# Fetching the next query tile back one step later, in a kernel whose SyncE queue carries copies and transposes alike

## The chip, the cores and the metric

The kernel runs on one core of one Trainium2 chip. The metric is the device time of one execution in microseconds (us). Times of a kernel are medians of several runs; profiles are single executions, and their span is about 2 us shorter than the device time of the same run.

The engines: PE is TensorE's matmul, PEld its weight loads, DVE is VectorE, ACT is ScalarE, POOL is GpSimd, SP or SPq is SyncE, which here issues almost every DMA from one queue.

## The reference, cut to what matters

One transformer block with linear attention, over 2048 tokens of width 576, 32 heads of 18:

```python
h = layernorm(x) * (1 + ca) + sa
q, k, v = heads(h @ wqkv)
phi_q = concat(softmax(q @ w_phi), softmax(-(q @ w_phi)))     # 36 features per head
phi_k = ...                                                   # the same of k
num = phi_q @ (phi_k^T v);  den = phi_q @ sum(phi_k)
x = x + ga * ((num / den) @ wo)
h = layernorm(x) * (1 + cb) + sb
x = x + gb * (relu(h @ w1) @ w2)                              # width 4608
```

The tokens are cut into 16 tiles of 128. The MLP at the end works on two tiles at a time: 8 blocks.

## The kernel before

First comes a phase that builds phi_k^T v and the query features of all tiles (up to some 91 us). Features of tiles 4 to 15 are not kept in SBUF until they are wanted: they are written to DRAM (`eqd`) and fetched back into a ring `EL` of NL = 3 buffers. Then the 8 MLP blocks run, each a first linear layer (`l1`, lines L673 and L680) and a second (`l2`, L735). The attention of tiles t+2 and t+3 is laced into the first layer of the block of tiles t and t+1.

What the change touches:

```python
NEQ, NE, NV, NL = 6, 5, 4, 3     # NL: buffers of the ring EL

def eq(u):                       # tiles 0..3 stay in SBUF, later ones live in the ring
    return EQ[:, SLOT[u], :] if u < QF else EL[:, u % NL, :]

def q_in(u):                     # L337: fetch of 288 KB, overwrites the buffer of tile u - 3
    sp.dma_start(EL[:, u % NL, :], eqd[:, u, :])

def q_turn(u):                   # L348: reads the buffer of tile u
    sp.dma_start_transpose(ET[:, u % NET], eq(u).rearrange("p (c f) -> p c f", f=P))

def q_fin(u):
    q_sm(u)                      # DVE: sums of the exponentials, reciprocal
    q_pool(u)                    # POOL: normalises in place
    q_turn(u)

def q_next(q):
    if q < NT:
        q_fin(q)
        if q + NL < NT:
            q_in(q + NL)         # waits, in the SyncE queue, for q_turn(q) just above

def attend(t):
    num_mm(t, pr)                # L389: matmuls on ET of tile t
    num_o(t, pr)                 # DVE: division, into o_sb
    if t > 1:
        act.activation(out=o_sb[:, t % 2, D:640], in_=o_sb[:, t % 2, 512:D], func=ACT.Copy)   # L795
    turn_dma(oT[:, t % 2], o_sb[:, t % 2, :])        # L401: transpose of the attention output
# wo_rest (L802) and wo_full (L808): matmuls on oT, by @ wo
```

Where the calls stand, block b with t0 = 2b + 2:

```python
# in l1 of block b
if (g, u) in (((0, 0), (1, "first")) if b == 1 else ((0, 0), (0, 2))):
    attend(t0 + int(u in (2, "first")))
if b == 0 and (g, u) == (1, "first"):
    q_next(t0 + 2)
if g and u == "rest":
    wo_rest(t0 + g - 1, pair(3))
# ... wo_full, residual, statistics, norm2 (a transpose of xn) ...
# in l2 of block b
if pos in ((4, 10) if b else (12,)):
    q_next(t0 + 2 + int(pos > 4))
# the output stores: L765 of tile t+1 ahead of pos 12, L769 of tile t behind it
```

So `q_next` is called for tile 4 in the first layer of block 0, for tile 5 at the end of block 0, for tiles 6 and 7 in the second layer of block 1, and so on, in pairs.

The softmax here doesn't subtract the row's maximum and nothing guards it: scores larger than these inputs give would overflow.

Of the kernel before, what the change touches and what calls it, by code (L numbers as in the profile page):

```python
# [17 lines left out]
NT = S // P  # L18
# [43 lines left out]
def tile_block(ctx, tc, a, out):  # L62
# [22 lines left out]
    NEQ, NE, NV, NL = 6, 5, 4, 3  # L85
# [250 lines left out]
    def q_in(u):  # L336
        sp.dma_start(EL[:, u % NL, :], eqd[:, u, :])  # L337
# [12 lines left out]
    def q_fin(u):  # L350
        q_sm(u)
        q_pool(u)
        q_turn(u)
# [427 lines left out]

    NB = NT // 2

    def q_next(q):
        if q < NT:
            q_fin(q)
            if q + NL < NT:
                q_in(q + NL)

    def attend(t):  # L790
        pr = pair(3)
# [25 lines left out]
    for b in range(NB):  # L817
# [3 lines left out]
        def in_l1(g, u):  # L821
            if not more:
                return
# [6 lines that stand above are left out]
            if g and u == 0:  # L830
                t = t0 + g - 1
                wo_full(t, pair(3))
                add_res(t, pair(3))
                bn(1, t)
            if (g, u) == (1, 2):
                norm2(b, t0)

        def in_l2(pos):
            if not more:
                return  # L840
            if pos == 1:
                norm2(b, t0 + 1)
            if pos == (8 if b else 12):
                hb = h2[:, (b + 1) % 2]
                for ci in range(NC):
                    dve.tensor_scalar(out=hb[:, ci, :], in0=hb[:, ci, :], scalar1=mod2[:, 1, ci:ci + 1],
                                      scalar2=mod2[:, 0, ci:ci + 1], op0=ALU.mult, op1=ALU.add)
            if pos in ((4, 10) if b else (12,)):
                q_next(t0 + 2 + int(pos > 4))
# [107 lines left out]
```

## Time and profile before

| | before |
|---|---|
| three runs, us | 389.54, 389.95, 391.97 (median 389.95) |
| span of the profiled run, us | 387.8 |
| TensorE busy, us | 380.5 (98%) |
| first layer of block 1, start to end, us | 23.33 |
| the same of blocks 2 to 5, us | 21.28 each |

The page and the views are read as follows. A line of the list of waits names the engine and line that waited, what ended the wait, then the total in us, the number of waits and the longest. A line of the timeline has the start, the length, the engine, the line of the kernel and what it writes from what. The length of an entry of SPq is the time in which SyncE issues the DMA; the data lands later (the fetch at 135.94 is issued in 0.33 us and lands 3.2 us after issue). The chain of waits goes back from the last instruction to what released each step. The granted clock is the share of TensorE's full clock that the trace records, as a mean over a window or a whole run: 1.00 is full speed, 0.50 is half.

The wait as TensorE has it, in its timeline:

```profile
137.88 0.83 PE L680 MATMUL PS<-h,R 64*128 64x256 bf16 x12
140.58 0.30 PE L802 MATMUL PS<-wo_sb,oT 64*128 64x288 bf16 x2 [1.87 <-DMA oT<-o_sb]
```

The twelve matmuls of L680 start at 137.88. What comes next in program order, L802, starts 2.70 us after that; the 1.87 us in brackets is idle time that ended when the DMA of oT landed.

### The profile page before, as it was taken

The page shows a single profiled execution, that of the slowest core. Times are in us where ns is not written, and L with a number is a line of the kernel's source. Part 1 is how long each engine was busy: PE and PEld are TensorE (multiplying, and loading weights), DVE is VectorE, ACT ScalarE, POOL GpSimd, SP SyncE. Part 2 cuts the span into 40 slices and gives each one's busy share as a digit, 9 for nine tenths or more (in the row PEclk, how much of TensorE's full clock was granted, in tenths as well). Part 3 has the DMA queues.
Part 4 walks back from the last instruction along what each step waited for, and adds up shares of the span by engine and source line. Part 5 has one row for each costly group of instructions (what it writes and reads, how often), then busy time and mean ns, then how long its engine had stood idle before and what let it go on. Part 6 is the DMA issues. An engine that isn't in the chain of part 4 may idle for free.

```text
span 387.8 us, 8927 instructions
## 1 busy us (share of the span) xinstructions
PE 380.5 (98%) x3705; PEld 310.3 (80%) x3705; DVE 242.7 (63%) x470; ACT 156.8 (40%) x380; POOL 125.3 (32%) x195
## 2 busy tenths in 40 slices
PE   8999999999999989999999999999999999999996
PEld 4887778888887868788888888887888788878885
DVE  2898998784897646735664485468365735552243
ACT  2689997687530233023302430341144114302510
POOL 2188889820107300530061026004500440042023
PEclk9999999999999999999999999999999999999999
DMA  7995799798520334151125104510530221200001
GB/s 296 421 417 207 275 379 362 134 260 290 67 63 19 47 79 35 33 137 28 29 63 108 36 19 91 96 19 19 123 36 19 45 64 36 35 0 33 3 0 33
DMA packets 48940, 43.18 MB, mean 111 GB/s; under 512 B 39297, under 2 KB 41986, under 8 KB 48130
## 3 DMA queue, kind: packets, MB, share of 16 engines
q1 hardware_dynamic: 48610, 42.41, 40.2%
q8 instruction: 29, 0.48, 0.5%
q10 hardware_dynamic: 288, 0.19, 0.2%
q14 instruction: 13, 0.11, 0.1%
HBM read 27.38 MB, written 5.90 MB: 86 GB/s over the span
## 4 chain that ended last, share of the span: by engine, by line
PE 90%; ACT 5%; DVE 2%; DMA 1%; issue 1%; POOL 1%; POOLq 0%; DVEq 0%; ACTq 0%
PE PS L673 32%; PE PS L735 31%; PE PS L272 11%; PE PS L680 5%; PE PS L808 4%; ACT RT L277 3%; PE PS L233 2%; PE PS L389 2%; PE PS L322 1%; DMA oT<-o_sb 1%; PE PS L249 1%; PE PS L406 1%; PE PS L802 0%; PE PS L257 0%; ACT RT L511 0%
## 5 line engine op out<-in xcount | busy, mean ns | idle before, releaser
L673 PE MATMUL PS<-h,R 128*128 128x256 bf16 x1152 | 132.1, 273 | 0.0
L673 PEld LDWEIGHTS <-R 128*128 128x128 bf16 x1152 | 111.6, 98 | 13.9 <-issue 0.6
L735 PEld LDWEIGHTS <-RH 128*128 128x128 f16 x846 | 82.8, 98 | 20.6
L721 POOL TENSOR_TENSOR yt<-yt,gb_row 128x288 f32<-128x288 f32 x23 | 28.0, 1219 | 204.7 <-DVE yt L720 204.7
L687 ACT ACTIVATE RH<-PS 128x256 f16<-128x256 f32 x72 | 27.5, 382 | 112.6 <-PE PS L680 92.3
L735 PE MATMUL PS<-R,RH 128*128 128x288 bf16 (+1 forms) x558 | 72.1, 286 | 0.0
L689 DVE SCALAR_TENSOR_TENSOR RH<-PS,RH 128x256 f16<-128x256 f32 x72 | 28.6, 412 | 61.0 <-ACT RH L687 61.0
L688 ACT ACTIVATE RH<-PS 128x512 f16<-128x512 f32 x72 | 42.9, 596 | 5.5 <-PE PS L673 4.6
L277 ACT ACTIVATE RT<-PS,rs 128x576 bf16<-128x576 f32 x64 | 42.8, 741 | 2.4 <-PE PS L272 1.8
L735 PE MATMUL PS<-RT,RH 128*128 128x288 f16 x288 | 37.9, 286 | 0.0
L739 ACT ACTIVATE RS<-PS 128x288 f32<-128x288 f32 x24 | 9.8, 410 | 65.2 <-PE PS L735 65.2
L272 PE MATMUL PS<-RH,R 116*128 116x288 bf16 x240 | 32.4, 286 | 0.0
L272 PE MATMUL PS<-RH,RT 116*128 116x288 bf16 x240 | 31.9, 286 | 0.3
L720 DVE TENSOR_TENSOR yt<-PS,RS 128x288 f32<-128x288 f32 x23 | 10.5, 455 | 31.0 <-PE PS L735 21.9
L238 DVE BATCH_NORM_STATS2 st<-x_sb 128x6 f32<-128x288 bf16 x64 | 25.9, 447 | 3.7 <-DMA x_sb<-in_xk_dram 3.1
L272 PEld LDWEIGHTS <-RT 116*128 116x128 bf16 x240 | 22.9, 98 | 6.0 <-issue 0.5
L272 PEld LDWEIGHTS <-R 116*128 116x128 bf16 x240 | 22.7, 98 | 5.9 <-issue 0.2
L722 POOL TENSOR_TENSOR x_sb<-yt,x_sb 128x288 bf16<-128x288 f32 x31 | 22.6, 731 | 2.9 <-DVE yt L718 1.1
L282 DVE TENSOR_REDUCE Rk<-RT 128x64 f32<-128x1152 bf16 x16 | 21.3, 1337 | 0.9 <-ACT RT L277 0.7
L282 DVE TENSOR_REDUCE Rq<-RT 128x64 f32<-128x1152 bf16 x16 | 21.5, 1344 | 0.0
L411 DVE TENSOR_TENSOR x_sb<-x_sb,PS 128x576 bf16<-128x576 bf16 x16 | 12.1, 753 | 13.4 <-PE PS L808 12.3
L680 PE MATMUL PS<-h,R 64*128 64x256 bf16 x288 | 19.9, 271 | 0.0
(119 smaller groups left out, 420.4 us busy)
## 6 DMA issues: line engine op xcount, KB each, us to landing
R<-in_w1a_dram SPq DMA_DIRECT2D x4, 1152.0 KB, 8.2
eqd<-RT SPq DMA_DIRECT2D x12, 288.0 KB, 2.1
RT<-eqd SPq DMA_DIRECT2D x12, 288.0 KB, 3.2
R<-in_w2b_dram SPq DMA_DIRECT2D x2, 1296.0 KB, 8.5
R<-in_w2a_dram SPq DMA_DIRECT2D x3, 864.0 KB
out_dram<-x_sb SPq DMA_DIRECT2D x15, 144.0 KB, 1.7
RT<-in_xT_dram SPq DMA_DIRECT2D x2, 640.0 KB, 13.9
x_sb<-in_xk_dram SPq DMA_DIRECT2D x3, 288.0 KB
```

The lines of the kernel that those rows point to most:

```text
L238: dve.bn_stats(out=s[:, hf, :], in_=x_sb[:, t, hf * HD:(hf + 1) * HD])
L272: pe.matmul(pr[:, k, 0:HD], lhsT=xt(t, ck), rhs=w[0:R, ck, k * HD:(k + 1) * HD], start=(ck == 0), stop=(ck == NC - 1))
L277: act.activation(out=E.rearrange("p (b h s e) -> p b h s e", b=2, s=2, e=DH)[:, :, :, s, :], in_=pr[:, :, 0:HD].rearrange("p b (h e) -> p ...
L282: dve.tensor_reduce(out=Rr, in_=E.rearrange("p (c e) -> p c e", e=DH), axis=AXX, op=ALU.add)
L673: pe.matmul(PS[:, 2 * u + hf, n * 256:n * 256 + 256], lhsT=w1a[:, ci, jj * P:(jj + 1) * P], rhs=hb[:, ci, :], start=(n == 0 and ci == 0), ...
L680: pe.matmul(PS[:, 2 * u + hf, n * 256:n * 256 + 256], lhsT=w1b[b0:b0 + 64, j * P:(j + 1) * P], rhs=hb[b0:b0 + 64, 4, :], start=False, stop ...
L687: act.activation(out=A11[:, j, :], in_=lo[:, :, 0, :], func=ACT.Relu)
L688: act.activation(out=A2[:, j, :, :], in_=PS[:, 2 * u + 1, :].rearrange("p (n s f) -> p n s f", n=2, s=2), func=ACT.Relu)
L689: dve.scalar_tensor_tensor(out=U3[:, j, :], in0=lo[:, :, 1, :], scalar=0.0, in1=A11[:, j, :], op0=ALU.max, op1=ALU.subtract)
L721: pool.tensor_tensor(out=y, in0=y, in1=gb_row[:, c], op=ALU.mult)
L722: pool.tensor_tensor(out=x_sb[:, t, c], in0=y, in1=x_sb[:, t, c], op=ALU.add)
L735: pe.matmul(PS[:, bank, 0:HD], lhsT=am[:, j, :], rhs=bm[:, j, :], start=first and j == 0, stop=(j % 9 == 8), skip_group_check=True)
```

## The change

The intent: the fetch of the next tile waits for the transpose of the present one, and the stores and transposes behind it in the SyncE queue wait with it. Fetched one call later, it finds its buffer free.

```diff
     NB = NT // 2
 
+    held = []
+
     def q_next(q):
+
+        if held and held[0] < NT:
+            q_in(held[0])
+        del held[:]
         if q < NT:
             q_fin(q)
-            if q + NL < NT:
-                q_in(q + NL)
+            held.append(q + NL)
```

## The prediction

> **What bounds the kernel now.** I read the page first, for which engine sets the end.
>
> ```profile
> span 387.8 us, 8927 instructions
> ...
> PE 380.5 (98%) x3705; PEld 310.3 (80%) x3705; DVE 242.7 (63%) x470; ACT 156.8 (40%) x380; POOL 125.3 (32%) x195
> ...
> PE 90%; ACT 5%; DVE 2%; DMA 1%; issue 1%; POOL 1%; POOLq 0%; DVEq 0%; ACTq 0%
> ```
>
> The reader is to see that TensorE is busy for 380.5 of 387.8 us. All that is not TensorE work is some 7.3 us, start-up and the last eviction and store included. A change that only moves DMA issues can win no more than what of those 7.3 us is a wait for a DMA. Which that is, the list of TensorE's waits over the whole run tells.
>
> ```profile
> PE PS L802 <- DMA oT<-o_sb: 1.9, 1, 1.9
> PE PS L233 <- POOL eps_t L225: 1.3, 1, 1.3
> PE PS L257 <- ACT RT L277: 0.2, 1, 0.2
> ```
>
> One wait in the MLP phase, 1.9 us, once: the first matmul of the output projection (L802) waits for the transposed attention output oT. Everything else there runs back to back. The same shows from another side when the first half of each MLP block (the first linear layer with the attention of two later tiles laced in) is put beside its like, with the busy times of the engines in windows cut at the block edges that the chain of waits gives:
>
> ```profile
> 91.25:112.60 21.35, 21.35 (x223) 17.91 (x222) 15.41 (x30) 11.11 (x25) 1.42 (x2) 1.00 0.59 142
> 128.03:151.36 23.33, 21.46 (x223) 17.85 (x221) 12.47 (x29) 8.35 (x21) 2.84 (x4) 1.00 0.46 60
> 166.79:188.07 21.28, 21.28 (x222) 17.87 (x221) 10.77 (x26) 8.36 (x21) 1.55 (x3) 1.00 0.35 80
> 203.50:224.78 21.28, 21.28 (x223) 17.86 (x221) 10.76 (x26) 8.36 (x21) 1.56 (x3) 1.00 0.34 66
> ```
>
> (The columns: window, its length, then busy time and count of PE, PEld, DVE, ACT and POOL, the granted clock, the DMA share, GB/s.) Block 1 takes 23.33 us, its like 21.28: 2.05 us more, at the same clock of 1.00. Blocks 2 to 5 are already equal to their TensorE work, to the hundredth. Last, the SyncE queue and its waits around that gap:
>
> ```profile
> 127.25 0.34 SPq L765 DMA_DIRECT2D out_dram<-x_sb  x1
> 131.32 1.29 SPq L348 DMA_TRANSPOSE RE<-RT  x1
> 135.94 0.33 SPq L337 DMA_DIRECT2D RT<-eqd  x1
> 136.36 0.39 SPq L769 DMA_DIRECT2D out_dram<-x_sb  x1
> 136.84 2.63 SPq L401 DMA_TRANSPOSE oT<-o_sb  x2
> ```
>
> ```profile
> SPq L337 <- DMA RE<-RT: 3.3, 1, 3.3
> ```
>
> This is the mechanism that the change is aimed at. At 131.32 SyncE issues the transpose of query tile 5 (L348). The next entry, the fetch of tile 8 (L337), overwrites the buffer that this transpose reads, so it waits 3.3 us for it. Behind it stand the output store L769 and the transpose of oT. The timeline shows the data of that oT ready much earlier: the last writer of o_sb (ACT, L795) runs from 133.55 for 0.26, to 133.81, and the store's data (POOL, L722) is there at 132.06 + 0.73 = 132.79. So oT was issued 136.84 - 133.81 = 3.0 us after its data, and TensorE, done with L680 soon after 138, had to wait until 140.58.
>
> [...] the 3.3 us stand in the SyncE queue and nothing behind is issued meanwhile. [...] the 0.33 us of L337 or 1.2 us of L401 aren't the transfer; for that I use the page's times from issue to landing (oT 2.6 median, 2.6 to 3.9; the query transpose 3.2 to 12.8, median 3.8; the fetch 2.7 to 3.6). [...] the granted clock is 1.00 in that window, so there is no second gain from a warmer clock.
>
> **The change part by part.** It removes nothing: the same twelve fetches of 288 KB, the same transposes, no instruction of a compute engine. It moves nine fetches (tiles 7 to 15) one call of q_next later, and puts them ahead of that call's own sums and transpose instead of behind them. The guard keeps fetches past tile 15 out.
>
> Call of tile 4 (block 0, SyncE at 103 us): its fetch, issued at 107.76, goes. Behind it stands a transpose of xn, issued at 109.14 and bound by its own data (xn is written from 108.48 for 0.64). No TensorE wait hangs on it: worth 0.
>
> Call of tile 5 (the end of block 0): now the fetch of tile 7 comes first. It waits for the transpose of tile 4, done since before 107.76, so it goes out right after the store at 127.25, at about 127.7, and by its landing time of 3.2 lands at about 131, before tile 5's transpose is issued. That transpose is bound by POOL (L289, 130.13 + 1.17 = 131.30) and stays at 131.32. Then no fetch. The store L769 goes at about 132.8, and oT at 133.83 instead of 136.84. With the landing of 2.6 to 3.9 it is there between 136.4 and 137.7. TensorE wants it at: L680 starts at 137.88, and in block 2 L802 starts 177.31 - 176.64 = 0.67 after L680, so at 138.55. It lands 0.8 to 2.1 us early, and the wait is gone. Now 140.58 - 137.88 = 2.70; then 0.67; gain 2.03 us. The block lengths gave 2.05.
>
> Later calls come in pairs. The first of a pair (tiles 6, 8, ...) now fetches ahead of its own sums, waiting for nothing. The second fetches behind a transpose that was issued some 5 us before and still has to wait for it, until 165.83 in block 1, just as the old first fetch did there; but that wait ends about when the second tile's own work is ready on POOL (165.03 + 1.16 = 166.19), so it holds nothing. What goes is the old second fetch (170.07 in block 1) in front of two stores. Behind these oT is issued at 172.59, 0.02 after its data (L795, 172.31 + 0.26), so the queue was not what held it, and TensorE has no gap. Worth 0.
>
> Lead: a fetch now has two calls instead of three before its first reader. Calls are 5 to 32 us apart, two of them over 30, and a fetch takes about 3.2: no new wait. The last stage (block 7) has no call: unchanged.
>
> Sum: -2.0 us for the one wait, 0 for the rest: 389.95 - 2.0 = 387.95.
>
> **Rivals.** First: tile 5's own transpose becomes what TensorE waits for. Its numerator matmuls (L389) start their weight loads at 135.99, and the old fetch that waited for the very same transpose went out at 135.94; the slack may be under 0.1 us. Today nothing else is in flight while it runs. After the change a store of 144 KB and oT are issued behind it at 132.8 and 133.8. If they stretch it, L389 starts late. For it: the slack, and that oT's landing was itself stretched to 3.7 (136.84 to 140.53) beside a fetch and a store. Against it: in windows of the DMA view the transpose's data moves from about 132.6 to 134.3, so most is through before the new traffic starts. I give it one in four, at 0.3 to 1 us: a time of 388.3 to 389.
>
> Second: oT itself lands late again, since it now runs close behind the query transpose. It would need 4.7 us from issue (133.83 to 138.55), more than any oT took (3.9). One in eight, costing up to 1 us.
>
> Third: the wait moved nowhere useful, for oT is held by something else than the fetch, and the time stays at 389.7. The order of the queue speaks against it: only the store stands between, and its data is there at 132.79. One in twelve.
>
> Fourth: the fetch that is now early in a call delays the transpose of xn (block 1, issued at 153.16) by sharing the DMA engines. The reader of that one, L846, starts at 159.19, 6 us after: covered. One in thirty that any of it shows.
>
> **Range and chances.** The centre is 388.0: the sum of 387.95, a little more for the first rival, a little less since the profiled run of before was 389.69, under its median. The three runs of before spread from 389.54 to 391.97, so one stray run adds up to 2 us. Eight in ten: 387.2 to 389.5. A gain of 2% would be 7.8 us, more than all the time in which TensorE isn't busy; a loss of 2% would need four new waits like the one removed. So within 2% is nearly sure: faster 0.01, same 0.98, slower 0.01.
>
> **What would show it.** TensorE's list of waits should have lost the line of L802; the stretch from L673 to L735 in block 1 should be 21.3 us instead of 23.33, all later blocks unchanged. In the SyncE queue the fetch should stand at about 127.7, and oT's transpose at about 133.8, right behind a store. The waits of L337 on RE should fall from 21.4 us in 9 waits to about half, those of the second calls. The prediction is wrong if L389 shows a wait in its place, if oT is still issued after 136, or if any block from 2 on grows over 21.28.

The sum came to 389.95 - 2.0 = 387.95, with -2.0 for the one wait, 0 for the rest and nothing for the clock. That a gap of 2 us is too short to lower the clock was the assumption and is shown by nothing here.

## The result, and the profile after

| | before | after |
|---|---|---|
| runs | 6 | 6 |
| median, us | 389.77 | 388.04 |
| lowest to highest, us | 389.54 to 391.97 | 387.79 to 388.24 |
| span of the profiled run, us | 387.8 | 386.3 |
| first layer of block 1, us | 23.33 | 21.28 |

The ratio is 0.9945, with a 95% interval of 0.9923 to 0.9967. Ratios here are the mean time of one kernel's fast runs over that of the other's of the same rounds, so not quite the ratio of the medians, which is 388.04 / 389.77 = 0.9956. That the two differ by 0.1% has a cause, and it comes up below.

The changed kernel is five lines longer, so L795 of before is L800, L802 is L807 and L808 is L813. First, the head of its page:

```profile
span 386.3 us, 8923 instructions
...
PE 379.6 (98%) x3705; PEld 309.7 (80%) x3705; DVE 242.6 (63%) x470; ACT 156.7 (41%) x380; POOL 125.3 (32%) x195
```

The same work on each engine, in 1.5 us less. TensorE's waits over the whole run:

```profile
PE PS L233 <- POOL eps_t L225: 1.3, 1, 1.3
PE PS L249 <- DMA R<-in_wsc_dram: 0.5, 1, 0.5
PE PS L434 <- DMA R<-in_wkT_dram: 0.3, 1, 0.3
PE PS L257 <- ACT RT L277: 0.2, 1, 0.2
```

The wait for oT is not there any more. The four that are left belong to the first phase. The busy times by engine in the first layers of blocks 1 and 2 (columns as in the prediction):

```profile
128.16:149.44 21.28, 21.28 (x222) 17.84 (x221) 12.46 (x29) 8.36 (x21) 2.84 (x4) 1.00 0.46 66
164.87:186.15 21.28, 21.28 (x223) 17.84 (x221) 10.77 (x26) 8.36 (x21) 1.55 (x3) 1.00 0.29 66
```

Block 1 now takes as long as its TensorE work, like the others. The SyncE queue around the old gap:

```profile
127.38 0.34 SPq L765 DMA_DIRECT2D out_dram<-x_sb  x1
127.81 0.39 SPq L337 DMA_DIRECT2D RT<-eqd  x1
131.45 1.29 SPq L348 DMA_TRANSPOSE RE<-RT  x1
132.95 0.46 SPq L769 DMA_DIRECT2D out_dram<-x_sb  x1
133.96 5.51 SPq L401 DMA_TRANSPOSE oT<-o_sb  x2
```

The fetch (L337, now that of tile 7) stands ahead of the query transpose and goes out at once. Behind the transpose the store and oT follow as soon as their data is there: ACT writes the last of o_sb at 133.94 (L800, 133.68 + 0.26), oT goes out at 133.96. Before it went out at 136.84, so it is 2.88 us earlier, or 3.0 measured from the start of the block. (The 5.51 us cover both transposes of oT, the second of which waits for its data in between.) TensorE in its timeline:

```profile
138.01 0.83 PE L680 MATMUL PS<-h,R 64*128 64x256 bf16 x12
138.67 0.29 PE L807 MATMUL PS<-wo_sb,oT 64*128 64x288 bf16 x2
```

From the start of L680 to the output projection 0.66 us, where it was 2.70.

Where the 1.5 us of the two spans come from: between the start of block 1 and the point where the matmuls of L735 leave the chain of waits in the last block, 251.69 us (128.03 to 379.72) became 249.64 (128.16 to 377.80), so 2.05 us less. Block 1 starts 0.13 later, in a run whose first loads came a little later. From the issue of the last store to the end of the span it is 2.84 us instead of 2.42. That is 2.05 - 0.13 - 0.42 = 1.50. The 0.42 is scatter: over the traces of all the kernels that last stretch lies between 2.39 and 3.07 us. The 2.05 is that of these two traces; what it is over more of them comes in the part on the prediction.

What is left of the waits of the fetch in the SyncE queue, before:

```profile
SPq L337 <- DMA RE<-RT: 21.4, 9, 3.6
```

and after:

```profile
SPq L337 <- DMA RE<-RT: 9.3, 4, 3.6
```

Only the four second calls of a pair still wait for a transpose.

### The profile page after: what moved, and what is told of

Its sections match the earlier page's. It is cut to its first block, busy times and chain, and to the rows that moved or that the text cites. A ratio compares the mean times of both kernels' runs of the same rounds, so it can differ in the third digit from the quotient of the medians.

```text
span 386.3 us, 8923 instructions
## 1 busy us (share of the span) xinstructions
PE 379.6 (98%) x3705; PEld 309.7 (80%) x3705; DVE 242.6 (63%) x470; ACT 156.7 (41%) x380; POOL 125.3 (32%) x195
## 4 chain that ended last, share of the span: by engine, by line
PE 87%; DMA 4%; ACT 4%; DVE 3%; issue 1%; POOL 1%; SPq 0%; POOLq 0%; DVEq 0%
PE PS L673 33%; PE PS L735 31%; PE PS L272 9%; PE PS L680 5%; PE PS L813 4%; ACT RT L277 3%; DMA x_sb<-in_xk_dram 2%; PE PS L389 2%; DMA R<-in_wkT_dram 2%; PE PS L322 1%; DVE Rk L282 1%; PE PS L406 1%; DVE st L238 1%; ACT RT L511 0%; PE PS L807 0%
## 5 line engine op out<-in xcount | busy, mean ns | idle before, releaser
L673 PE MATMUL PS<-h,R 128*128 128x256 bf16 x1152 | 132.1, 273 | 0.0
L673 PEld LDWEIGHTS <-R 128*128 128x128 bf16 x1152 | 111.4, 98 | 14.1 <-issue 0.6
L735 PEld LDWEIGHTS <-RH 128*128 128x128 f16 x846 | 82.7, 98 | 20.7
L735 PE MATMUL PS<-R,RH 128*128 128x288 bf16 (+1 forms) x558 | 72.1, 286 | 0.0
L735 PE MATMUL PS<-RT,RH 128*128 128x288 f16 x288 | 37.9, 286 | 0.0
L680 PE MATMUL PS<-h,R 64*128 64x256 bf16 x288 | 19.9, 271 | 0.0
```

The costliest lines, as they stand in the source:

```text
L673: pe.matmul(PS[:, 2 * u + hf, n * 256:n * 256 + 256], lhsT=w1a[:, ci, jj * P:(jj + 1) * P], rhs=hb[:, ci, :], start=(n == 0 and ci == 0), ...
L680: pe.matmul(PS[:, 2 * u + hf, n * 256:n * 256 + 256], lhsT=w1b[b0:b0 + 64, j * P:(j + 1) * P], rhs=hb[b0:b0 + 64, 4, :], start=False, stop ...
L735: pe.matmul(PS[:, bank, 0:HD], lhsT=am[:, j, :], rhs=bm[:, j, :], start=first and j == 0, stop=(j % 9 == 8), skip_group_check=True)
```

## The experiments

The theory to be tested: the whole gain is one hold, that of the oT transpose in block 1 behind the fetch of tile 8, and the eight other moves are worth nothing. Its rivals: many small gains; DMA traffic beside oT rather than the hold; and, later, something that the medians hide.

### One fetch alone moved

```diff
 # the kernel before
     def q_next(q):
+        if q == 6:
+            q_in(8)
         if q < NT:
             q_fin(q)
-            if q + NL < NT:
+            if q + NL < NT and q != 5:
                 q_in(q + NL)
```

> The kernel before, with one fetch alone moved: tile 8's, from behind the transpose of tile 5 to the head of the call of tile 6. The other eight stay where they were. Theory (the whole gain is the one hold of the oT transpose in block 1): the same as the full change, 388.0 us, 1.7 to 1.8 under the kernel before, ratio 0.9945 to 0.9960, no wait of TensorE on oT, block 1's first half 21.3 us. Rival (the gain is the sum of shorter holds or less DMA traffic in many calls): at most a third of it, 389.2 to 389.7.

Measured: 387.97 us (387.83 to 388.10, 6 runs), ratio to the kernel before 0.9934 (0.9913 to 0.9956); no wait of TensorE on oT, block 1's first layer 21.45 us (128.26 to 149.71, cut from the chain of waits). The 0.17 us over 21.28 are a late start of L389, which comes up below. The SyncE queue still waits 18.4 us in 8 waits for query transposes at a fetch, nearly as long as the kernel before, and the time is that of the full change. The ratio is lower than I had expected because four of the eleven reference runs were at 391.3 to 391.9; more of that below.

### The other eight moved

```diff
 # the changed kernel
             q_fin(q)
-            held.append(q + NL)
+            if q == 5:
+                q_in(8)
+            else:
+                held.append(q + NL)
```

> The changed kernel with tile 8's fetch put back where it was, behind the transpose of tile 5 and ahead of the store and of oT; the other eight are moved. Theory: nothing is left of the gain, 389.7 us, ratio 0.999 to 1.001, TensorE waits 1.9 us for oT as before. Rival (many calls each give a little): 388.2 to 388.6.

Measured: 390.15 us (389.77 to 390.55, 6 runs), ratio 0.9991 (0.9968 to 1.0013). TensorE's wait is back:

```profile
PE PS L810 <- DMA oT<-o_sb: 1.8, 1, 1.8
```

Nothing of the gain is left. The median is 0.45 over the expected 389.7; by the ratio the kernel and the one before can't be told apart. The two runs together settle the first rival: one fetch of nine carries all of it.

### The traffic without the hold

In the kernel before, the fetch of tile 8 did two things to oT: it held the queue, and its 288 KB then moved just ahead of oT's data. This run has the traffic alone.

```diff
 # the changed kernel
-    mask = small([P, KVW], BF16, "mask")
+    mask = small([P, 2 * D], BF16, "mask")
-    load(sp, mask[:], "mask")
+    load(sp, mask[:, 0:KVW], "mask")
             held.append(q + NL)
+            if q == 5:
+                sp.dma_start(mask[:], eqd[:, 8, :])
```

> The changed kernel plus one extra fetch of 288 KB at the old place of tile 8's, into a buffer that nobody reads any more, so that it waits for nothing: the traffic of the old order without its hold. Theory (the hold is what cost): the fetch goes out at about 132.8, the store at 133.2, oT still at 134.0; even with the landing of 3.7 us that oT had beside the old fetch it is there at 137.7, before 138.6: no wait on oT, 388.0 to 388.3 us. Rival (it was the traffic beside oT): oT lands 1 us or more late, a wait of 0.5 to 1 us, 388.6 to 389.2. If the query transpose itself is stretched by traffic behind it, a wait of L389 shows instead, up to 0.5 us.

Measured: 388.10 us (387.88 to 388.44), ratio 0.9936 (0.9912 to 0.9960), no wait on oT. The SyncE queue of this run:

```profile
131.62 1.29 SPq L348 DMA_TRANSPOSE RE<-RT  x1
132.97 0.57 SPq L795 DMA_DIRECT2D mask<-eqd  x1
133.63 0.39 SPq L769 DMA_DIRECT2D out_dram<-x_sb  x1
134.14 5.70 SPq L401 DMA_TRANSPOSE oT<-o_sb  x2
```

With all of the old traffic in front of it (432 KB in two DMAs), oT still went out at 134.14 and was in time. Traffic alone costs nothing here.

### The hold without the traffic

```diff
 # the changed kernel
             held.append(q + NL)
+            if q == 5:
+                sp.dma_start(EL[0:16, 8 % NL, 0:256], eqd[0:16, 8, 0:256])
```

> The changed kernel plus a fetch of 8 KB at the old place of tile 8's, into the buffer that tile 5's transpose reads, so that it waits as the old one did: the hold without the 288 KB. Theory: the queue stands until about 136.0, oT goes out at about 136.9 and lands 2.6 to 3.0 us later, at 139.5 to 139.9 against the 138.6 that TensorE wants: a wait of 0.8 to 1.3 us, 388.9 to 389.3 us. The rest of the 2.05 us is then the traffic's share (landing 3.7 instead of about 3). Rival (traffic alone): no wait, 388.0 us. Rival (hold alone, traffic costs nothing): the full 1.9 to 2.0 us, 389.7.

Measured: 388.91 us (388.63 to 389.33), ratio 0.9959 (0.9937 to 0.9981), that is 0.87 over the changed kernel. TensorE's timeline:

```profile
137.85 0.83 PE L680 MATMUL PS<-h,R 64*128 64x256 bf16 x12
139.44 0.30 PE L809 MATMUL PS<-wo_sb,oT 64*128 64x288 bf16 x2 [0.76 <-DMA oT<-o_sb]
```

From L680 to the projection 1.59 us, against 0.66 without a hold and 2.70 with the full fetch. In the chain of waits oT takes 2.59 us from issue (136.80) to landing (139.39), where before it took 3.69. So the gap of 2.03 us divides into 0.92 for the hold and 1.11 for the traffic that the hold had put right in front of oT. The second part exists only because of the first: the run above has the traffic without the hold, and there oT's spare time covered it. The split is that of single traces. The five traces of the kernel before have gaps of 1.78 to 2.03 us, so the traffic's part lies between 0.86 and 1.11; by the medians of all runs it is 0.88 for each part (388.03 without the hold, 388.91 here, 389.79 before, without the slower runs that come up below).

### Each fetch one call later still

```diff
 # the changed kernel
-        if held and held[0] < NT:
-            q_in(held[0])
-        del held[:]
+        if len(held) > 1:
+            u = held.pop(0)
+            if u < NT:
+                q_in(u)
```

> The changed kernel with each fetch one call later still: tile 7's at the head of the call of tile 6, and so on, so that every fetch finds its buffer free long before. SyncE's waits for the query transpose at a fetch (9.3 us in 4 waits in the changed kernel) fall to 0. Theory: those waits hold nothing that TensorE waits for, so 388.0 us, ratio to the changed kernel 0.999 to 1.001. Rival (fewer waits in the queue are worth time by themselves): 387.5 or less. Second rival (too little lead now, one call, at the least some 5 us): a wait of DVE for the fetch, and over 388.5.

Measured: 387.97 us (387.79 to 388.33), ratio to the kernel before 0.9941 (0.9919 to 0.9963). The waits of L337 for query transposes are all gone from the SyncE queue, 9.3 us of them, and the time is the same. A lead of one call is enough, too: VectorE's list of waits has none for a fetch. So these 9.3 us of waiting in the queue were worth nothing: TensorE waited for none of what stood behind them.

### How near the next wait is

The prediction's first rival was that the numerator matmuls (L389) of tile 5 would begin to wait for its query transpose. A small fetch that waits for that transpose, put where it holds nothing, shows when SyncE sees it landed.

```diff
 # the changed kernel, in attend
         turn_dma(oT[:, t % 2], o_sb[:, t % 2, :])
+        if t == 4:
+            sp.dma_start(EL[0:16, 8 % NL, 0:256], eqd[0:16, 8, 0:256])
```

> The changed kernel with a fetch of 8 KB into the buffer that tile 5's transpose reads, placed behind the first transpose of oT, so that it holds nothing that matters: it goes out when tile 5's transpose has landed, with the store and oT in flight behind that. It tells how near the changed kernel is to a wait of the numerator matmuls (L389, weight loads from 136.1). Theory: landing at 135.9 to 136.1, a slack of under 0.2 us, no wait of TensorE, 388.0. Rival (the late landing of before was the queue's, not the transpose's): the probe goes out right behind the first oT transpose, at 135.3 or so.

Measured, one look: 388.57 us (a single run, from which no verdict on the time follows). The probe in the SyncE queue:

```profile
134.06 1.29 SPq L401 DMA_TRANSPOSE oT<-o_sb  x1
136.45 0.34 SPq L803 DMA_DIRECT2D RT<-eqd  x1
```

The transpose had landed at 136.45, later than I expected: the weight loads of L389 wanted to start at 136.20, when those of L673 before them ended, and started at 136.48. The same wait shows in TensorE's timeline of the run with one fetch moved:

```profile
136.49 0.41 PEld L389 LDWEIGHTS <-RE 128*128 128x128 bf16 x10 [0.27 <-DMA RE<-RT]
```

Measured from the end of the weight loads before it, L389 starts 0.02 us after them where it doesn't wait. In the five traces of the kernel before it started 0.02 us after them four times and 0.17 us once. In the six traces of kernels without the hold it was 0.02 us twice and 0.11, 0.28, 0.28 and 0.30 us in the others (the last is the run with the extra traffic). So there is no slack at all at this place, and the landing scatters by some 0.3 us. It costs a little: in the three traces with 0.28 to 0.30 us the first layer of block 1 takes 21.45 or 21.46 us, in the other three without the hold 21.27 or 21.28. Whether the traffic that now follows closely makes it later can't be told from so few.

### A second group of runs

In the first comparison one of six runs of the kernel before was at 391.97, and in the next four of eleven were over 391, while no run of the changed kernel or its variants without the gap was. All of these count as fast runs. So the kernel before was run against itself.

> The kernel before, unchanged (one comment line more), against itself. Of its 17 timed runs so far 12 took 389.5 to 390.3 us and 5 took 391.3 to 392.0; none of the 30 runs of the changed kernel and its variants shows such a second group above its first. If the second group belongs to this kernel, one or two of these six runs are at 391.3 to 392 and the ratio is 0.998 to 1.002; if it belongs to how the reference runs were taken (a kernel's turn among others), none of the six is. A profile that falls in the second group would show a longer wait for oT in block 1 (3.5 us instead of 1.9), or a wait elsewhere.

Measured: 389.56 us (389.49 to 391.47), ratio 0.9991 (0.9967 to 1.0015); one of its six runs was in the second group (391.47, clock 0.996). The group belongs to the kernel.

> The kernel before once more, for its profile and one time: 389.5 to 390.3 us with a wait of 1.9 us for oT, or, in about three of ten, 391.3 to 392 with what makes the second group.

Measured: 389.84 us, in the first group, with a wait of 1.9 us for oT. It shows nothing of the second.

To bring the second group out, TensorE's gap was made longer.

```diff
 # the kernel before
-    mask = small([P, KVW], BF16, "mask")
+    mask = small([P, 2 * D], BF16, "mask")
-    load(sp, mask[:], "mask")
+    load(sp, mask[:, 0:KVW], "mask")
             if q + NL < NT:
                 q_in(q + NL)
+            if q == 5:
+                sp.dma_start(mask[:], eqd[:, 8, :])
```

> The kernel before with one more fetch of 288 KB (into a buffer that nobody reads any more) behind tile 8's, ahead of the store and oT: oT lands about 1.1 us later, so TensorE's gap grows from 1.9 to about 3 us. Of 35 runs of the kernel before, 8 were at 391.3 to 392.0 and each of those had a mean granted clock of 0.996, where all others had 0.998 to 1.000; none of 25 runs without the gap was so. Theory: the gap itself lets the granted clock drop in a share of the runs, a share that grows with its length: more than half of the six runs (perhaps all) have 0.996 or less and lie 1.7 us above the rest, at about 392.5 to 393, the rest at 390.8 to 391.2; the trace of such a run shows the lower clock in the few us right after the gap. Rival (the second group has another cause, such as the run's place or another stage): one or two of six at most, as before, all shifted by 1.1 us.

(A slip in this text: the clock was on record for seven of those eight runs; the run at 391.97 of the first comparison had none listed.)

Measured: 391.24 us median, ratio 1.0022 (0.9998 to 1.0046); the six runs are 390.08, 390.37 and 390.66 with a clock of 1.0, and 391.81, 392.16 and 392.19 with 0.996. The gap grew less than expected: the wait for oT was 2.4 us, not 3. Three of six are in the second group, where it was about a quarter before. That lies between what the theory (more than half) and the rival (one or two) expected, and six runs are too few to show that the share grew: with no difference between the kernels, so many would come by chance once in six (Fisher's exact test, 3 of 6 against 12 of 53, 0.17). What settles more is that the profiled run is in the group. TensorE's waits, and its granted clock (the third column from the end) in windows around the gap:

```profile
PE PS L804 <- DMA oT<-o_sb: 2.4, 1, 2.4
```

```profile
140.50:141.00 0.50, 0.00 (x0) 0.00 (x0) 0.00 (x0) 0.00 (x0) 0.00 (x0) 1.00 1.16 219
141.00:141.20 0.20, 0.00 (x0) 0.00 (x0) 0.00 (x0) 0.00 (x0) 0.00 (x0) 0.70 1.23 269
141.20:141.40 0.20, 0.00 (x0) 0.00 (x0) 0.00 (x0) 0.00 (x0) 0.00 (x0) 0.50 1.27 177
141.40:144.40 3.00, 2.84 (x13) 1.74 (x14) 0.35 (x1) 0.00 (x0) 0.00 (x0) 0.50 0.04 7
144.40:144.60 0.20, 0.20 (x4) 0.14 (x2) 0.20 (x1) 0.00 (x0) 0.00 (x0) 0.77 0.00 0
```

The clock falls to half at 141.08 (a share of 0.4 of the window at full speed and the rest at half gives 0.70), some 2.0 us after TensorE went idle at 139.1, and comes back at 144.49 (0.54 at full speed and 0.46 at half give 0.77): 3.41 us at half clock, 2.93 of them after the matmuls had begun again at 141.56, so about 1.5 us lost. The first projection shows it in TensorE's timeline:

```profile
141.56 0.42 PE L804 MATMUL PS<-wo_sb,oT 64*128 64x288 bf16 x2 [2.43 <-DMA oT<-o_sb]
141.91 2.10 PE L810 MATMUL PS<-wo_sb,oT 128*128 128x288 bf16 x8
```

Those eight matmuls take 1.15 us in a run at full clock. The first layer of block 1 takes 25.27 us here (128.43 to 153.70), which is 3.99 over 21.28: 2.60 of it is the gap (from L680 to the projection 3.27 instead of 0.67), the rest of 1.4 the clock. And 3.41 us at half clock in a span of 390.3 make a mean clock of 0.996, the figure that every run of the second group has.

> The kernel before for one more trace, in the hope of one in its second group (8 in 35 so far). If it is there: 391.3 to 392.0 us, clock 0.996, [...]. Else 389.5 to 390.3.

> As the look before this one: second group with the clock drop right after the gap of block 1, or 389.5 to 390.3 us with none.

Measured: 389.50 and 390.30 us, both in the first group, waits of 1.6 and 1.7 us for oT, and full clock around them. So no trace of the kernel before in its second group exists, and that its clock fell at the same place is inferred from the run with the longer gap, not shown. What is shown is the count. Of 53 runs of the kernel before with a recorded clock, 12 lie between 391.21 and 392.01, all with a mean clock of 0.996, and 41 between 389.41 and 390.62, all with 0.998 to 1.000 (in the third look at the kernel before, the 0.998 comes from the last 2.5 us alone, clock 0.72, when no matmul is left and nothing is lost). Of 31 runs of kernels without the gap none has 0.996 and none is over 388.6. Were the share the same in both, so uneven a count would have a chance of 0.2% (Fisher's exact test, 0 of 31 against 12 of 53). The runs with a gap of 1.8 us (the other eight moved) had none in six, which a share of 12 in 53 allows with a chance of 0.2.

From the last matmul to the end of the span TensorE is idle for 3.6 to 4.3 us. In windows of 0.3 us, the clock falls to half there after 2.2 to 2.4 us in four of the fourteen traces (two of them of the kernel before), once after 3.7, and in the other nine not at all; the changed kernel's trace keeps the full clock through 4.05 us. So in the unchanged kernel, too, little over 2 us of idle time was enough for half clock in some runs, while in others much more was not. Nothing is lost at that place, as no matmul is left.

### A buffer at the end

With the gap gone, the time in which TensorE is idle lies at the start and at the end. This was a try at the end, on top of the change.

```diff
 # the changed kernel, the last two products of l2
-            dve.tensor_tensor(out=yt[:, 0, c], in0=PS[:, bank, c], in1=gb_row[:, g], op=ALU.mult)
-            dve.tensor_tensor(out=x_sb[:, t, g], in0=yt[:, 0, c], in1=yl[:, c], op=ALU.add)
+            dve.tensor_tensor(out=SS[:, 2, c], in0=PS[:, bank, c], in1=gb_row[:, g], op=ALU.mult)
+            dve.tensor_tensor(out=x_sb[:, t, g], in0=SS[:, 2, c], in1=yl[:, c], op=ALU.add)
```

> The changed kernel with one more edit, at its end, where the trace of the changed kernel still has time in which TensorE is idle: the last two products of the second linear layer write their scaled half to a buffer that is free by then (SS, part 2) instead of yt, which POOL still reads (L722) until 382.19. The first of them then starts when its matmuls are done, at about 381.1 instead of 382.22, and only the second is left behind the last matmul (382.25): its two VectorE steps end at about 382.9 instead of 383.44, so the last store goes out some 0.5 us earlier: 387.5 us, ratio to the changed kernel 0.9985 to 0.999. Rival (the last store is bound by something else, such as the stores before it on the queue at 382.2 and 382.6): 387.9 to 388.1.

Measured: 388.04 us (387.96 to 388.42), ratio to the kernel before 0.9947 (0.9925 to 0.9969): the same as the change alone. The timeline of its end:

```profile
382.25 0.33 SPq L765 DMA_DIRECT2D out_dram<-x_sb  x1
382.31 0.31 DVE L778 TENSOR_TENSOR RS<-PS,gb_row 128x144 f32<-128x144 f32 x1
382.62 0.43 SPq L772 DMA_DIRECT2D out_dram<-x_sb  x1
382.65 0.31 DVE L779 TENSOR_TENSOR x_sb<-RS,RE 128x144 bf16<-128x144 f32 x1
383.51 0.34 SPq L780 DMA_DIRECT2D out_dram<-x_sb  x1
```

The data is ready at 382.96, some 0.5 us earlier, as planned; the last store still goes out at 383.51, as in the changed kernel (383.46). So the rival held, that the store isn't bound by its data. L772 is issued until 383.05; what the 0.46 us from there to 383.51 are, no line of the trace names, and it stays open.

## Why the prediction was right, and where it was not

The time was predicted at 388.0 with a range of 387.2 to 389.5, and came to 388.04. By its own steps:

**The bound and the one wait: right.** The wait of L802 on oT was the only one in the MLP phase, and it alone was removed. Moving one fetch of the nine gives all of the gain, moving the other eight none.

**The size of the gain: right in the two traces, a little too large for the kernel, and the centre helped by luck.** 2.03 us were expected from L680 to the projection; it went from 2.70 to 0.66, so 2.04, and block 1 fell from 23.33 to 21.28. oT was to go out at 133.83 and land within 2.6 to 3.9 us; it went out at 133.96 and the DMA view gives 3.0 us to landing. But the profiled run of the kernel before has one of its longest gaps: over its five traces L680 to the projection is 2.45 to 2.70 us, 2.56 in the mean. From the start of block 1 to the last matmul of the run it is 256.00 us in the mean of those five and 254.17 in that of the six without the hold, so the usual gain is 1.83 us in the traces, near the 1.76 of the medians. Of the 0.20 that is missing, some 0.14 is that the mean gap is shorter (2.56 - 0.67 = 1.89) and some 0.07 the late start of L389. The sum came out all the same because its base, 389.95, was a median of three runs with one of the slower group among them, 0.16 above the 389.79 of the usual run: the two errors nearly cancel.

**Worth 0 for the call of tile 4, the later pairs and the tail: right**, by the run with the other eight moved. The second call of a pair was to wait as the old first one did: it issues its fetch at 163.96, which is the old 165.83 less the 2.05 us by which block 1 is shorter, plus the 0.13 of the later start, to 0.05.

**The first rival, given one in four at 0.3 to 1 us: there, but smaller.** The matmuls of L389 do run into a late landing of their query transpose, by at most 0.28 us over the usual, and once also in the kernel before. In three of six traces that made block 1 0.17 to 0.19 us longer; in the other three it cost nothing that shows.

**The second, third and fourth: did not show.** oT was in time even with all of the old traffic ahead of it; nothing but the fetch had held it; no transpose of xn was missed.

**The step that failed** is the sentence "so there is no second gain from a warmer clock". It rested on one profiled run with a clock of 1.00, and on the assumption, shown by no run, that a gap of 2 us is too short to matter to the clock. In about a quarter of the runs of the kernel before (12 of 53) the mean clock is 0.996, and those take 1.87 us longer by the medians of the two groups (391.66 and 389.79). The gap's removal takes this group away. So the change gives 1.76 us in the usual run (389.79 to 388.03, the median of the 31 runs without the gap) and in a mean over many runs some 0.42 more (12/53 of 1.87). That is the difference between the ratio of medians, 0.9956, and that of means, 0.9945. The "stray run" of 391.97 that the prediction put down to scatter was one of that group by its time. The prediction's number still came out, because it was a median.

What stays open: whether the clock falls at this gap in the second group of the kernel before (no trace of it exists), how much of the 1.87 us is the clock (the trace with the longer gap shows 1.4 to 1.5), and what sets which runs fall into the group.

## What to carry to other kernels

In a queue that one engine issues in order, as SyncE does here (nothing went out behind the fetch in the 3.3 us that it waited), ask of each entry that waits what stands behind it and who is the next to need that; total waiting time says little (18.4 us of it remained in the run that had the whole gain, and taking away the last 9.3 gave none). Ask also what the transfer of the entry that waits will run beside: here its 288 KB moved right ahead of the urgent one, which landed in 3.69 us instead of the 2.59 behind a held 8 KB, and that doubled the price (0.92 us for the hold, 1.11 for the traffic, in single traces). And when a kernel's runs fall into two groups, look at the clock of each run before calling the upper one scatter: here a wait of 1.6 to 1.9 us in TensorE cost about its own length (1.76 us by the medians), and 12 of 53 runs, all with a mean clock of 0.996, took 1.87 us more.

## What the runs show of the hardware

- The clock and TensorE's idle time: half clock (0.50) began about 2.0 us after TensorE went idle in the traced gap with 2.4 us of wait, and lasted 3.41 us. After the last matmul it began at 2.2 to 2.4 us in four of fourteen traces and at 3.7 in one, while 4.05 us of idle time left the clock at full in the changed kernel's. What decides between these, no run here shows. A mean clock of 0.996 is on record for none of 31 runs without a gap, none of 6 at 0.8 us of wait, none of 6 at 1.8 (the other eight moved), 12 of 53 at 1.6 to 1.9 (the lower clock there not traced), 3 of 6 at 2.4.
- A DMA that waits, and those behind it: while the fetch waited 3.3 us, SyncE issued nothing else. The transpose of 128 x 640 elements behind it went out at 136.84 instead of 133.96, and it landed in 2.59 us behind a held fetch of 8 KB and in 3.42 to 3.69, over five traces, behind a held one of 288 KB (a store of 144 KB between in both).
- The scatter of a landing: the DMA transpose of 128 x 1152 elements in block 1 came at the same point of the program, but up to 0.28 us later in some runs than in others, and 2.39 to 3.07 us passed from the issue of the last store to the end of the span.
